# Top-k attention and two MLPs on one core: query transposes moved in the queue, a second buffer for probability halves, and the last weight's upper halves moved from GpSimd to ScalarE

## The chip, the cores and the metric

One core of a Trainium2 chip runs the whole program in one launch. The metric is the device time in microseconds (us) of one execution. Of the kernel before, three runs and one profiled execution are at hand.

## The reference, cut to what matters

```python
# attention: B=4, H=8, S=576, D=64
scores = scale * np.matmul(q, k.transpose(0, 1, 3, 2))
kth = np.partition(scores, -top_k, axis=-1)[..., -top_k:-top_k + 1]   # top_k = 32
scores = np.where(scores >= kth, scores, -1e9)
attn = np.exp(scores - max);  attn = attn / (attn.sum() + 1e-09)
x = np.matmul(attn, v)                     # -> 2304 tokens x 512
# first MLP, 512 -> 2048 -> 512
h = x @ w_in1;  x = (h * sigmoid(h)) @ w_out1
# second MLP, 512 -> 2048 -> 512
h = x @ w_in2;  out = np.where(h > 0, h, exp(min(h, 0)) - 1) @ w_out2
```

## The kernel before, in words

The work is cut into 18 chunks of 128 tokens, and each chunk into 8 attention tiles (one head, 128 queries, 576 keys), 144 tiles in all. Two of the chunks gather the 64 left-over queries of two batches; their tiles hold two heads each. Every operand of a matmul is carried as two float16 halves, an upper half `hi` and a rest `lo`, so a product is three matmuls.

A loop over slots writes out by hand, in `slot`, the program order of every engine; nothing is rescheduled. Slot s holds, for attention, the top-k of tile s on VectorE (`topk_ops`, four MAX8 and three MATCH_REPLACE8, then the mask L592), the upper probability halves of tile s-1 on ScalarE (`emit_ehi`, L618), the rests of tile s-2 on GpSimd and their transposing DMA (`emit_elo`, L624 to L627), the product with V of tile s-3 on TensorE (`emit_av`, L646), and the scores of tile s+1 on TensorE (`emit_qk`, L532). From slot 13 on a slot can also hold a quarter of a chunk's first MLP, from slot 25 on of the second, so that from then on each slot has one quarter: `emit_in` (48 matmuls, L702), `emit_act` (three or four activations on ScalarE, L716 to L724), then one slot later `emit_g` on GpSimd (L730), `emit_ghi` on ScalarE (L734) and `emit_glo` on GpSimd, and two slots later `emit_out` (12 matmuls, L750). On TensorE a slot runs: input matmuls of the MLP, product with V, output matmuls, scores of the next tile.

The names and lines that the change touches:

- `e16_p` is a pool with one buffer. `emit_ehi` writes tile t's upper halves into it, `emit_elo` the rests beside them, and the transposing DMA `et<-e16` (L627) reads both. So ScalarE's L618 of the next tile waits until that DMA has landed.
- `q_tp` (L511, L516) issues the transposing DMA `qt<-qd` for a pair of tiles from a copy of the queries in DRAM, on SP's queue, where all DMAs of the program are issued in order. It stands in the list `late[2g-3]` as a second function, which `slot` runs at the start of the slot after, behind that slot's `et` DMA.
- `kd`, `vd` and `qd` (L418, L424, L498) are the stores of split keys, values and queries to DRAM. They share one buffer, `k16_p`: ScalarE's next split into it (L389, L448, L486) waits until the store has landed.
- `w_split` makes the halves of the second MLP's output weights (weight 3, 16 blocks of 128 x 512) on GpSimd: L336 the upper half, then L164 the rest. `w_scaled` scales the block on ScalarE a slot earlier (L161). `spread` gives the slots of the blocks: slots 14 to 28 before.
- Weights live in one SBUF tile `W` of 66 rows. The raw block n lies two rows above its halves, so rows 64 and 65 are free once the last block has been split.
- The values of batch 1 are prepared `d` slots after the keys, by a table of `(r, d)`.

Of the kernel before, what the change touches and what calls it, by code (L numbers as in the profile page):

```python
# [11 lines left out]
F16 = mybir.dt.float16  # L12
# [4 lines left out]
ALU = mybir.AluOpType  # L17
# [15 lines left out]
def kernel(  # L33
# [11 lines left out]
    nc = tc.nc  # L45
    B, H, S, D = q.shape
    NT, DM = out.shape
# [15 lines left out]
    def pool(name, bufs, **kw):  # L63
        return ctx.enter_context(tc.tile_pool(name=name, bufs=bufs, **kw))
# [9 lines left out]
    e16_p = pool("e16", 1)  # L74
# [19 lines left out]
    WEND = 4 * NWP + OFF  # L94
    W = const.tile([128, WEND, 2 * DM], F16, name="W")
    Wraw = W.bitcast(F32)
    Wi = W.bitcast(I32)
    Wh = W.bitcast(BF16)

    chunks = []  # L100
    for b in range(0, B, 2):
# [58 lines left out]
    def scaled(x, s):  # L160
        nc.scalar.activation(out=x, in_=x, func=AF.Copy, scale=s)  # L161

    def sub(dst, x, hi):
        nc.gpsimd.tensor_tensor(dst, x, hi, op=ALU.subtract)  # L164
# [87 lines left out]
    def w_raw(j, n, w=None):  # L252
        return (Wraw if w is None else w)[:, j * NWP + n + OFF, :]
# [56 lines left out]
    def w_hi(j, n):  # L310
        nc.scalar.activation(out=W[:, j * NWP + n, 0:DM], in_=w_raw(j, n), func=AF.Copy, scale=sW[j][0])
# [16 lines left out]
        pmul(kc[:, 1:2], kc[:, 0:1], sW[2][1])  # L328

    def w_scaled(j, n):  # L330
        scaled(w_raw(j, n), sW[j][0])

    def w_split(j, n):
        x = j * NWP + n
        raw = w_raw(j, n)
        nc.gpsimd.tensor_scalar(W[:, x, 0:DM], raw, 1.0, 0.0, op0=ALU.mult, op1=ALU.add)  # L336
        sub(W[:, x, DM:2 * DM], raw, W[:, x, 0:DM])


    knat, vnat, qnat, kT, qT, vT, qsc = {}, {}, {}, {}, {}, {}, {}  # L340
# [273 lines left out]
    e16s = {}  # L614

    def emit_ehi(t):
        h = e16_p.tile([128, 2 * S], F16, tag="e16", name="e16")
        nc.scalar.activation(out=h[:, 0:S], in_=e32s[t], func=AF.Copy)  # L618
        e16s[t] = h

    def emit_elo(t):
        e = e32s.pop(t)
        h = e16s.pop(t)
        nc.gpsimd.tensor_tensor(h[:, S + LO:2 * S], e[:, 0:SF], h[:, 0:SF], op=ALU.subtract)  # L624
        nc.gpsimd.tensor_tensor(h[:, S:S + LO], e[:, SF:S], h[:, SF:S], op=ALU.subtract)  # L625
        et = et_p.tile([128, 2 * FC + 1, 128], F16, tag="et", name="et")
        nc.sync.dma_start_transpose(out=et, in_=h)  # L627
        ets[t] = et
# [177 lines left out]

    LDA = -99
    LDB = 28  # L810
    LAG = 13
# [10 lines left out]
    loads, sumsq, tiny, early, splits, late, low, decs = (defaultdict(list) for _ in range(8))  # L822

    def prep(slots, load, total, reduce, ops, hi, lo):
        s0, s1, s2 = slots
        if reduce and s1 >= 0:
            s0, s1 = s0 - 1, s1 - 1
        loads[s0].append(load)

        def a():  # L830
            m = total()
            if reduce:
                due.append((m, lambda m: early[s2].append(lambda: ops(m=m))))
            else:
                tiny[s2].append(ops)

        sumsq[s1].append(a)
        late[s2].append((hi, lo))

    first = {b: min(t for (bb, _), t in first_use.items() if bb == b) for b in range(B)}  # L840
    for (b, i), t in first_use.items():
        x = dict(b=b, i=i)
        if b == 0:
            prep((t - 5, t - 4, t - 3), partial(k_load, **x), partial(k_sum, **x), True,
                 partial(k_ops, **x), partial(k_hi, **x), partial(k_lo, **x))
            late[t - 2].append((partial(k_tp, **x), None))
            prep((t - 1, t, t + 1), partial(v_load, **x), partial(v_sum, **x), True,
                 partial(v_ops, **x), partial(v_hi, **x), partial(v_lo, **x))
        else:
            d, r = 4, first[b] - 35 + 8 * i + 2 * (b % 2)  # L850
            if b == 1:
                r, d = ((16, 2), (21, 3), (27, 3), (32, 3))[i]
            prep((r - 1, r + 1, r + 2), partial(k_load, **x), partial(k_sum, **x), True,
                 partial(k_ops, **x), partial(k_hi, **x), partial(k_keep, **x))
            late[t - 3].append((partial(k_tp, **x), None))
            r += d
            prep((r - 1, r + 1, r + 2), partial(v_load, **x), partial(v_sum, **x), True,
                 partial(v_ops, **x), partial(v_hi, **x, keep=True), partial(v_keep, **x))
            loads[t].append(partial(v_back, **x))
    for ch in range(NCH):  # L860
        t = ch * H
        y = t - 3
        if ch:
            y = t - 4 if ch == 1 else t - 5 if chunks[ch - 1][1] == 0 and ch > 2 else t - 8
        x = (y - 3 if ch > 1 else y - 2, y - 1, y)
        prep(x, partial(q_load, ch), partial(q_sum, ch), False,
             partial(q_ops, ch), partial(q_hi, ch), partial(q_lo, ch))
        for g in range(t // 2, (t + H) // 2):
            late[2 * g - 3].append((None, partial(q_tp, g)))

    wload, wnow = defaultdict(list), defaultdict(list)

# [2 lines left out]
    def spread(s, counts):  # L875
        return {(n, None): s + x for n, x in enumerate(x for x, c in enumerate(counts) for _ in range(c))}
# [5 lines left out]
    for j, d in dec.items():  # L882
        end = max(d.values()) + 1
        for x, s in d.items():
            decs[s].append((j, *x))
        grams[end - (j < 3)].append(j)
        traces[end + (j == 3)].append(j)
        held.add(end + (j == 3))
        if j == 3:
            for (n, _), x in spread(end + 1, (1, 1, 1, 2, 1, 2, 1, 1, 1, 1, 1, 1, 0, 1, 1)).items():  # L890
                late[x].append((partial(w_scaled, j, n), None))
                splits[x + 1].append(partial(w_split, j, n))
            continue
        ends.append(end)
# [45 lines left out]
    def slot(s):  # L940
# [25 lines left out]

        if LDA <= s < LDB:
            for f in loads[s - 1]:
                f()
        if 0 <= s - 2 < NTILE:  # L970
            emit_elo(s - 2)
        if not LDA <= s < LDB:
            for f in loads[s - 1]:
# [50 lines left out]
        if 0 <= s - 1 < NTILE:  # L1024
            emit_ehi(s - 1)
# [84 lines left out]
```

## Time and profile before

| | |
|---|---|
| median of 3 runs | 1146.91 us (1146.54 to 1148.77) |
| the profiled execution | 1149.13 us, span 1147.4 us |
| PE busy | 1011.7 us, 88% of the span |
| DVE busy | 952.2 us, 83% |
| ACT busy | 874.8 us, 76% |
| POOL busy | 820.7 us, 72% |
| DMA queue of the program | 387008 packets, 139.39 MB |

PE is TensorE's matmuls, PEld its weight loads, DVE is VectorE, ACT ScalarE, POOL GpSimd, and SP the engine whose queue issues the DMAs; SPq is that queue, and L12 is line 12 of the kernel. A row of a list of waits says which instruction waited for which, the time in total, how often and the longest. In a timeline a bracket gives the engine's idle time ahead of the instruction, and what ended it.

### The profile page before, as it was taken

How to read it: one execution, taken by the hardware profiler on the slowest of the kernel's cores; microseconds unless marked ns; L12 is line 12 of the kernel's file. 1: busy time of each engine (PE TensorE's matmuls, PEld its weight loads, DVE VectorE, ACT ScalarE, POOL GpSimd, SP SyncE). 2: the span in 40 equal slices, each digit the busy share in tenths (PEclk: the TensorE clock that was granted, in tenths of full speed). 3: DMA queues.
4: the chain of work that ended last, by engine and by line, in shares of the span. 5: the costliest groups of instructions: out<-in, count | busy, mean ns of one | idle time of the engine just before them, and what ended most of it. 6: DMA issues, size and time to landing. Idle time of an engine off the chain costs nothing.

```text
span 1147.4 us, 31015 instructions
## 1 busy us (share of the span) xinstructions
PE 1011.7 (88%) x11974; PEld 723.8 (63%) x11974; DVE 952.2 (83%) x2215; ACT 874.8 (76%) x1568; POOL 820.7 (72%) x1026
## 2 busy tenths in 40 slices
PE   0166779689999999999999999999999999999997
PEld 0123426376677676777777776767677777777765
DVE  5998998999798989999998989989889999994000
ACT  5566887789887888888888888877777778776654
POOL 5877875898877676777768776777667677767543
PEclk9978999899999999999999999999999999999999
DMA  9978792555688654646778565638665545433100
GB/s 308 298 211 244 237 227 48 110 115 100 127 159 158 106 121 92 129 96 119 119 138 158 98 117 101 120 83 135 109 127 84 94 84 88 83 61 61 29 13 17
DMA packets 387156, 141.37 MB, mean 123 GB/s; under 512 B 362944, under 2 KB 370112, under 8 KB 387008
## 3 DMA queue, kind: packets, MB, share of 16 engines
q1 hardware_dynamic: 387008, 139.39, 58.9%
q8 instruction: 94, 1.54, 0.6%
q14 instruction: 54, 0.44, 0.1%
HBM read 52.17 MB, written 21.10 MB: 64 GB/s over the span
## 4 chain that ended last, share of the span: by engine, by line
PE 29%; POOL 23%; DMA 12%; issue 11%; ACT 7%; SPq 2%; DVE 1%; POOLq 0%; ACTq 0%
PE h L702 13%; PE a L750 12%; DMA et<-e 8%; POOL e L624 7%; POOL t L730 6%; POOL gh L164 4%; PE S L532 2%; PE av L646 2%; POOL e L625 2%; ACT gh L734 1%; POOL x L164 1%; DMA qt<-qd 1%; POOL v L164 1%; DMA vd<-v 1%; ACT e L618 1%
## 5 line engine op out<-in xcount | busy, mean ns | idle before, releaser
L702 PE MATMUL h<-xt,W 128*128 128x128 f16 x6912 | 410.5, 219 | 2.0 <-DMA xt<-x 2.0
L750 PE MATMUL a<-W,gh 128*128 128x512 f16 x1728 | 402.6, 383 | 9.8 <-ACT o L796 4.9
L702 PEld LDWEIGHTS <-W 128*128 128x128 f16 x6912 | 395.6, 98 | 13.2 <-issue 2.8
L564 DVE MAX8 m<-r 128x8 f32<-128x576 f32 x432 | 312.7, 749 | 2.2
L750 PEld LDWEIGHTS <-gh 128*128 128x128 f16 x1728 | 160.5, 99 | 188.0 <-issue 11.5
L624 POOL TENSOR_TENSOR e<-e,e 128x512 f16<-128x512 f32 x144 | 166.9, 1159 | 137.5 <-ACT e L618 126.4
L164 POOL TENSOR_TENSOR gh<-t,gh 128x512 f16<-128x512 f32 x144 | 167.1, 1160 | 69.1 <-ACT gh L734 69.1
L568 DVE MATCH_REPLACE8 r<-m,r 128x576 f32<-128x576 f32 x288 | 213.7, 742 | 0.0
L730 POOL TENSOR_TENSOR t<-u,t 128x512 f32<-128x512 f32 x144 | 183.0, 1271 | 29.4 <-ACT u L724 23.1
L734 ACT ACTIVATE gh<-t 128x512 f16<-128x512 f32 x144 | 90.3, 627 | 119.1 <-POOL t L730 117.9
L564 DVE MAX8 m<-S 128x8 f32<-128x576 f32 x144 | 109.6, 761 | 56.5 <-PE S L532 55.9
L532 PE MATMUL S<-kt,qt 128*128 128x288 f16 (+1 forms) x640 | 98.7, 295 | 50.5 <-DVE sv L136 21.1
L579 ACT ACTIVATE e<-S,bias,c 128x576 f32<-128x576 f32 x144 | 119.7, 831 | 25.8 <-DVE r L568 18.7
L618 ACT ACTIVATE e<-e 128x576 f16<-128x576 f32 x144 | 97.5, 677 | 47.8 <-DMA et<-e 25.7
L532 PEld LDWEIGHTS <-qt 128*128 128x128 f16 (+1 forms) x640 | 55.9, 102 | 120.4 <-issue 23.8
L592 DVE SCALAR_TENSOR_TENSOR e<-S,m,e 128x576 f32<-128x576 f32 x144 | 115.3, 800 | 0.1
L568 DVE MATCH_REPLACE8 r<-m,S 128x576 f32<-128x576 f32 x144 | 107.5, 747 | 0.0
L646 PE MATMUL av<-vt,et 128*128 128x64 f16 (+1 forms) x2240 | 91.9, 195 | 16.3 <-DMA et<-e 15.8
L646 PEld LDWEIGHTS <-et 128*128 128x128 f16 (+1 forms) x2240 | 80.3, 102 | 27.4 <-DMA et<-e 21.1
L317 PE MATMUL lo<-W,eye 128*128 128x512 f32 x96 | 58.5, 694 | 20.0 <-ACT W L322 19.1
L280 POOL TENSOR_TENSOR W<-W 128x512 int32<-128x512 int32 (+1 forms) x55 | 69.0, 1278 | 9.3 <-DVE W L277 3.5
L724 ACT ACTIVATE u<-u,c 128x512 f32<-128x512 f32 x72 | 58.6, 814 | 2.4
(125 smaller groups left out, 1165.0 us busy)
## 6 DMA issues: line engine op xcount, KB each, us to landing
W<-in_moe_w_in_dram SPq DMA_DIRECT2D x32, 512.0 KB, 7.1
W<-in_moe_w_out_dram SPq DMA_DIRECT2D x22, 512.0 KB, 6.2
qd<-q SPq DMA_DIRECT2D x34, 256.0 KB, 4.3
kn<-in_k_dram SPq DMA_DIRECT2D x16, 288.0 KB, 4.1
qn<-in_q_dram SPq DMA_DIRECT2D x16, 256.0 KB, 3.6
out_dram<-o SPq DMA_DIRECT2D x16, 256.0 KB, 2.8
vd<-v SPq DMA_DIRECT2D x12, 320.0 KB, 4.3
vt<-vd SPq DMA_DIRECT2D x24, 160.0 KB, 2.7
```

What stands on the lines that cost most here:

```text
L164: nc.gpsimd.tensor_tensor(dst, x, hi, op=ALU.subtract)
L532: nc.tensor.matmul(out=ps[n * e:n * e + n, a, 0:HALF], lhsT=qt[:, 2 * (t % 2) + p, n * e:n * e + n], rhs=kt[:, a * HALF:(a + 1) * HALF], s ...
L564: nc.vector.max(st["m8"][:, i, :], src if i == 0 else st["r"])
L568: nc.vector.match_replace(out=fold(r) if i == 0 else r, in_to_replace=st["m8"][:, i, :], in_values=src if i == 0 else r, imm_value=LOW,)
L579: nc.scalar.activation(out=fold(e), in_=src, func=AF.Exp, scale=c[:, 0:1], bias=bias)
L592: nc.vector.scalar_tensor_tensor(e, src, st["m8"][:, n - 1, 7:8], e, op0=ALU.is_ge, op1=ALU.mult, accum_out=acc)
L618: nc.scalar.activation(out=h[:, 0:S], in_=e32s[t], func=AF.Copy)
L624: nc.gpsimd.tensor_tensor(h[:, S + LO:2 * S], e[:, 0:SF], h[:, 0:SF], op=ALU.subtract)
L646: nc.tensor.matmul(out=o, lhsT=et[:, c, n * e:n * e + n], rhs=r, start=(i == 0), stop=(i == len(seq) - 1))
L702: nc.tensor.matmul(out=ps[:, f:f + 128], lhsT=w, rhs=xt[:, z, :], start=(kk == 0 and x == 0), stop=(kk == KDM - 1 and x == 2),)
L730: nc.gpsimd.tensor_tensor(t, u, t, op=ALU.add if l else ALU.mult)
L750: nc.tensor.matmul(out=acc, lhsT=gh[:, z, u * 128:(u + 1) * 128], rhs=W[:, n, w * 512:(w + 1) * 512], start=(m == 0 and x == 0), stop=(m = ...
```

## The change

Four edits, of which the first three go by tables of slots and lists.

1. Query transposes of the pairs g > 4 are issued at the end of slot 2g-3, and no longer at the start of slot 2g-2.
2. Odd tiles from tile 31 on write their probability halves into rows 64 and 65 of `W` (`spare`) and not into the one buffer of `e16_p`, which leaves that buffer to the even tiles.
3. The upper halves of weight 3 are made by `w_hi` on ScalarE (L311, with the scale in it), in the slot of `w_scaled` and just ahead of it; L336 on GpSimd goes. The blocks are spread over slots 14 to 25, two in some.
4. The values of batch 1, heads 4 and 5, are prepared one slot later.

```diff
+    spare = W[:, WEND - 2:WEND, :].rearrange("p a x -> p (a x)")
...
     def w_scaled(j, n):
+        w_hi(j, n)
         scaled(w_raw(j, n), sW[j][0])
 
     def w_split(j, n):
         x = j * NWP + n
-        raw = w_raw(j, n)
-        nc.gpsimd.tensor_scalar(W[:, x, 0:DM], raw, 1.0, 0.0, op0=ALU.mult, op1=ALU.add)
-        sub(W[:, x, DM:2 * DM], raw, W[:, x, 0:DM])
+        sub(W[:, x, DM:2 * DM], w_raw(j, n), W[:, x, 0:DM])
...
     def emit_ehi(t):
-        h = e16_p.tile([128, 2 * S], F16, tag="e16", name="e16")
+        if t % 2 and t > TWO:
+            h = spare[:, 0:2 * S]
+        else:
+            h = e16_p.tile([128, 2 * S], F16, tag="e16", name="e16")
...
+    TWO = 30
...
-                r, d = ((16, 2), (21, 3), (27, 3), (32, 3))[i]
+                r, d = ((16, 2), (21, 3), (27, 4), (32, 3))[i]
...
-            late[2 * g - 3].append((None, partial(q_tp, g)))
+            late[2 * g - 3].append((partial(q_tp, g), None) if g > H // 2 else (None, partial(q_tp, g)))
...
-            for (n, _), x in spread(end + 1, (1, 1, 1, 2, 1, 2, 1, 1, 1, 1, 1, 1, 0, 1, 1)).items():
+            for (n, _), x in spread(end + 1, (2, 1, 2, 2, 2, 1, 2, 0, 1, 1, 1, 1)).items():
                 late[x].append((partial(w_scaled, j, n), None))
                 splits[x + 1].append(partial(w_split, j, n))
```

On SP's queue, around tiles 80 to 83 (chunk 10, in the middle of the program), the rows before: `et` is the transposed probabilities, `qt` the transposed queries, `xt` the MLP's transposed input, `kd` the stored keys.

```order
L627 DMA_TRANSPOSE et<-e_10328 128x9x128
L511 DMA_TRANSPOSE qt<-qd 128x4x128
L681 DMA_TRANSPOSE xt<-x_10447 128x8x128
L627 DMA_TRANSPOSE et<-e_10451 128x9x128
L627 DMA_TRANSPOSE et<-e_10576 128x9x128
...
L418 DMA kd<-k_10587 128x1152
L511 DMA_TRANSPOSE qt<-qd 128x4x128
L627 DMA_TRANSPOSE et<-e_10707 128x9x128
```

And the same place now:

```order
L630 DMA_TRANSPOSE et<-e_10303 128x9x128
L684 DMA_TRANSPOSE xt<-x_10422 128x8x128
L630 DMA_TRANSPOSE et<-W 128x9x128
L511 DMA_TRANSPOSE qt<-qd 128x4x128
L630 DMA_TRANSPOSE et<-e_10550 128x9x128
...
L418 DMA kd<-k_10561 128x1152
L630 DMA_TRANSPOSE et<-W 128x9x128
L511 DMA_TRANSPOSE qt<-qd 128x4x128
```

Each `qt` has moved: it stood behind an even tile's `et` and the stores of that slot, and stands now behind an odd tile's `et`. The transpose that followed `kd` in the first piece is, for its pair of tiles, the one ahead of `et<-e_10550` in the second. Odd tiles' `et` read `W`.

On ScalarE, behind the upper probability halves of tile 19 (slot 20, in the stretch where weight 3 is split), the rows before:

```order
L618 ACTIVATE e_2561<-e_2474 128x576
L161 ACTIVATE vn<-vn,sv 128x640
L448 ACTIVATE v_2576<-vn 128x10x64
L161 ACTIVATE W<-W,sw 128x512
L577 ACTIVATE bias<-m_2642,fixed,c 128x1
L579 ACTIVATE e_2649<-S,bias,c 128x576
```

And now:

```order
L621 ACTIVATE e_2567<-e_2483 128x576
L162 ACTIVATE vn<-vn,sv 128x640
L448 ACTIVATE v_2582<-vn 128x10x64
L312 ACTIVATE W<-W,sw 128x512
L162 ACTIVATE W<-W,sw 128x512
L312 ACTIVATE W<-W,sw 128x512
L162 ACTIVATE W<-W,sw 128x512
L577 ACTIVATE bias<-m_2651,fixed,c 128x1
L579 ACTIVATE e_2658<-S,bias,c 128x576
```

Three weight instructions more stand between tile 19's upper halves and tile 21's exponentials.

## Rows read from the trace of the kernel before

**Rows 1.** The page's part 2: the span in 40 slices, TensorE

```profile
PE   0166779689999999999999999999999999999997
```

**Rows 2.** Windows: length, then busy us (count) of PE, PEld, DVE, ACT, POOL; clock

```profile
0.00:245.00 245.00, 144.60 (x1186) 86.63 (x1187) 223.13 (x507) 171.93 (x316) 184.50 (x231) 0.91 0.77 204
311.00:1041.00 730.00, 708.73 (x8980) 525.84 (x8979) 667.32 (x1560) 587.39 (x1052) 524.44 (x670) 1.00 0.61 111
```

**Rows 3.** The chain that ended last: start, us, what; two output steps of the MLP

```profile
862.76 2.59 PE a L750 x12
...
868.95 2.59 PE a L750 x12
```

**Rows 4.** Waits of PE from 311 to 1041 us

```profile
PE av L646 <- DMA et<-e: 12.2, 13, 2.4
PE S L532 <- DMA qt<-qd: 5.6, 7, 1.7
PE a L750 <- ACT o L796: 2.9, 5, 0.8
```

**Rows 5.** Waits of ACT from 311 to 1041 us

```profile
ACT gh L734 <- POOL t L730: 86.7, 73, 1.9
ACT e L618 <- DMA et<-e: 15.4, 17, 3.9
ACT q L486 <- DMA kd<-k: 7.4, 4, 3.0
...
ACT q L486 <- DMA vd<-v: 6.5, 3, 2.3
```

**Rows 6.** L627, the transposing DMA of the probabilities, from 311 to 1041 us

```profile
DMA to landing us min/median/max: 3.2/3.3/5.1
```

**Rows 7.** Timeline of SP's queue around tile 74: start, us, what

```profile
601.65 1.29 SPq L627 DMA_TRANSPOSE et<-e  x1
...
605.70 1.25 SPq L511 DMA_TRANSPOSE qt<-qd  x1
```

**Rows 8.** Timeline of PE just behind it

```profile
610.21 0.67 PE L532 MATMUL S<-kt,qt 128*128 128x288 f16 x4 [1.67 <-DMA qt<-qd]
```

**Rows 9.** Timeline of PE at tile 97

```profile
759.05 0.85 PE L646 MATMUL av<-vt,et 128*128 128x64 f16 x14 [2.38 <-DMA et<-e]
759.72 4.17 PE L750 MATMUL a<-W,gh 128*128 128x512 f16 x12
```

**Rows 10.** Windows, the same columns, at that place

```profile
759.00:762.00 3.00, 2.94 (x20) 1.55 (x21) 1.33 (x3) 2.85 (x6) 2.15 (x3) 0.53 0.00 0
```

**Rows 11.** Groups of instructions: shapes, count | busy us, mean ns | idle before

```profile
L311 ACT ACTIVATE W<-W,sw 128x512 f16<-128x512 f32 x48 | 31.9, 719 | 0.0
...
L336 POOL TENSOR_SCALAR W<-W 128x512 f16<-128x512 f32 x16 | 9.9, 619 | 0.0
```

**Rows 12.** Windows of ACT alone: length, busy us (count), clock, DMA

```profile
187.00:236.00 49.00, 32.48 (x59) 0.86 0.51 101
```

**Rows 13.** Timeline of ACT at tiles 18 to 20

```profile
224.87 0.67 ACT L618 ACTIVATE e<-e 128x576 f16<-128x576 f32 x1
...
230.57 0.68 ACT L618 ACTIVATE e<-e 128x576 f16<-128x576 f32 x1 [0.29 <-DVE z L143]
...
235.77 0.71 ACT L161 ACTIVATE W<-W,sw 128x512 f32<-128x512 f32 x1
...
239.17 0.69 ACT L618 ACTIVATE e<-e 128x576 f16<-128x576 f32 x1
```

**Rows 14.** Timeline of PE at tile 20

```profile
244.72 0.58 PE L646 MATMUL av<-vt,et 128*128 128x64 f16 x14 [0.25 <-DMA et<-e]
...
246.71 2.33 PE L750 MATMUL a<-W,gh 128*128 128x512 f16 x10 [0.98 <-POOL gh L164]
```

**Rows 15.** Timeline of DVE a slot later

```profile
249.57 0.77 DVE L564 MAX8 m<-S 128x8 f32<-128x576 f32 x1 [1.00 <-PE S L532]
```

**Rows 16.** Timeline of PE in slot 31

```profile
301.61 4.44 PE L750 MATMUL a<-W,gh 128*128 128x512 f16 x12 [1.98 <-ACT o L796]
```

## The prediction

> **What bounds the kernel now.** I read the page's slices first: from about 230 us to the end TensorE's digit is 9 nearly throughout [rows 1]. The windows cut the span there. Up to 245 us DVE is busy 223.1 of 245 us, PE 144.6; from 311 us (tile 31) to 1041 us PE is busy 708.7 of 730, DVE 667.3 and ACT 587.4 [rows 2]. So there are two stages: the first goes at the pace of DVE's top-k, the second at TensorE's. In the chain of waits two output steps of the MLP follow each other in 6.19 us [rows 3]; where nothing disturbs TensorE, that is the length of a slot, and this change takes none of its matmuls away.
>
> What can be gained in the second stage is therefore what TensorE stands idle there: 730 - 708.7 = 21.3 us. The list of its waits names nearly all of it: 12.2 us for transposed probabilities, 5.6 for transposed queries, 2.9 for ScalarE's output copy, which frees the accumulator [rows 4]. One loss lies beside these. After the longest idle time, 2.38 us at tile 97, the granted clock was 0.53 for the next 3 us, between the two levels of 1.2 and 2.4 GHz, and the output step took 4.17 us, not 2.59 [rows 3, 9, 10]: 1.6 us more.
>
> The judgement that TensorE is the bound there can be doubted, since a busy share counts pipelined matmuls as full. The Trainium skill says so (Perfetto Trace Analysis, Identifying the Most-Contended Engine): judge TensorE's headroom by the share of weight loads. That is 525.8 of 730, 72% [rows 2], and would leave some 200 us of room. The undisturbed slots of 6.19 us speak against it, and they decide: I cap the gain at the idle time.
>
> **Edit 2, the second buffer.** It adds no instruction. ScalarE waited 15.4 us in 17 places for the last `et` to land before it could write the next upper halves [rows 5]. With alternating buffers it waits for the DMA of two tiles ago, a slot of 6.2 us earlier, against a flight of 3.2 to 5.1 us [rows 6]; those 15.4 us go. But ScalarE's far longer wait is for GpSimd, 86.7 us for `t` [rows 5]: upper halves, rests on GpSimd, `t`, `gh` and the activations form a ring through both engines that a buffer does not shorten. Part of TensorE's 12.2 us comes from the buffer, part from that ring and from slow transposes. Bounds: 0 and 12.2 us; I take 7, a little over half, since the stalls that cost ScalarE most (3.9 us the longest) are the buffer's. Of the clock's 1.6 us I take 1. ScalarE's output copy stands right behind the upper halves in its slot, so an earlier ScalarE frees the accumulator earlier: of 2.9 us I take 2 (bounds 0 and 2.9).
>
> **Edit 1, the query transposes.** Before, `qt` stands behind an `et` that waits for GpSimd, then behind loads and a store: at tile 74 it went out 4.05 us after that `et` [rows 7], and TensorE waited 1.67 us for it [rows 8]. It is now issued a whole `et` earlier, about 6.2 us, and the longest of these waits was 1.7 us [rows 4]. Its buffer is long free, since the scores that last read it were made a slot before. I take 5 of the 5.6 us (bounds 0 and 5.6).
>
> It has a price. It leaves an even tile's `et` and the stores `kd` and `vd`, and comes behind an odd tile's `et`. ScalarE's 13.9 us of waits for those two stores [rows 5] should shrink, which I leave within the 7 above. The odd `et` right after a chunk's start is one that TensorE waits for, and is now followed at once by another transpose. The trace does not show this pair. Its nearest rows bound what an `et` can lose: nothing, or 5.1 - 3.3 = 1.8 us [rows 6]. I take 0.25 us, near the median and not the longest, since two issues of 1.29 and 1.25 us [rows 7] put the second transpose some 2.5 us into a flight of 3.3. Some 13 chunks: 3 us lost. Where there was no stall, this costs nothing.
>
> The Trainium skill (DMA: Bandwidth & Descriptors, Issuing engines are not separate DMA queues) says that all DMAs run on the same 16 engines and interleave. By that rule the collision is only moved from even tiles to odd ones, and the saving would be nearer the third rival below than to mine; rows 6 shows that flights do stretch, but not by whom.
>
> **Edit 3, upper halves on ScalarE.** Off GpSimd go 16 instructions, 9.9 us; onto ScalarE go 16 of 0.719 us, 11.5 us [rows 11], all in slots 14 to 25, and in most of slots 14 to 20 three more in a row. GpSimd's saving is covered by its own waits. ScalarE's addition is not free: by the order, 15 of the 16 fall between 187 and 236 us, 10.8 us against 49 - 32.5 = 16.5 us of idle time there [rows 12], and part of that idle time is waiting that stays (for `et`, whose buffer is single until tile 31, and for stores). Follow tile 20: three more instructions stand at 235.77 us, 2.2 us, on top of 1 to 2 us of backlog, my estimate from the same rows. Its upper halves then start not at 239.17 us but 3 to 4 later [rows 13], and so does its `et`, for which TensorE already waits at 244.72 [rows 14]. The scores behind are waited for by DVE at 249.57 [rows 15], so this lies on the path: 3 to 4 us lost.
>
> Most is given back: from slot 26 on ScalarE has no weight work and GpSimd's slots 28 and 29 have none, and in slot 31 TensorE loses 1.98 us to a late output copy and 4.44 - 2.59 = 1.85 us in the step behind it [rows 3, 16]. Bounds: 5 lost, 4 gained; I take 1.5 lost. DVE's work is untouched.
>
> **Edit 4** moves one preparation by a slot; the work and its engines are the same. With edits 1 and 3 before 311 us it is inside the bounds just given. The early query transposes (before 187 us) lie under DVE's 223 us [rows 2]; if that cover went, they would cost one issue of 1.25 us each [rows 7] on SP.
>
> **The sum.** Gained 7 + 1 + 2 + 5 = 15, lost 3 + 1.5 = 4.5: 10.5 us. The profiled execution took 1149.13 us, 2.2 above the median; 1149.13 - 10.5 = 1138.6, and on the median 1146.91 - 10.5 = 1136.4 us.
>
> **The rivals**, on the median's scale.
>
> Full relief: the ring keeps pace once the buffer is gone, and all idle time that the rows name goes, 12.2 + 5.6 + 2.9 + 1.6 = 22.3 us, with the first stage even: 1124.6 us. For it: undisturbed slots run at 6.19 us. Against: the 86.7 us ring. If the weight-load rule of the skill were right, the gain could go beyond the cap; I give that no more than this rival's chance. 0.14.
>
> The ring bounds: the second buffer only moves ScalarE's wait from `et` to `t`. Then only the 5 us for queries are saved, less 1.5: 1143.4 us. For it: 86.7 against 15.4 us [rows 5]. 0.20.
>
> The collision eats it: each chunk's odd `et` loses about 0.9 us, 13 x 0.9 = 11.7 instead of 3, and the sum is 15 - 11.7 - 1.5 = 1.8 us gained: 1145.1 us, no change. 0.06.
>
> Slower: the odd `et` of each chunk stretches by the full 1.8 us, 13 x 1.8 = 23.4 us, on TensorE's path. 15 - 23.4 - 1.5 = -9.9: 1156.8 us. It decides from (15 - 1.5) / 13 = 1.04 us a chunk on. Against: the median flight of 3.3 us lies by the shortest, though many DMAs are in flight. 0.08, with ScalarE's 11.5 us falling wholly on the path counted in.
>
> That the change doesn't do what it says would need `spare` to wait for TensorE's reads of `W`; by the program order an odd tile's upper halves still wait for a DMA and for DVE alone. No chance of its own.
>
> **How the numbers follow.** A measurement of this kernel can tell 0.2%, 2.3 us, from no change. My forecast has 0.52; with full relief and the ring rival, both faster, 0.86; same 0.06, slower 0.08. The forecast's own bounds are about 1127 to 1143. The range 1124 to 1145 reaches from full relief over the ring rival to the edge of no change, and leaves out the slower cases, part of the same ones and the forecast's tails, under 2 in 10.
>
> **What would show it.** Right: ScalarE's wait for `et` after 311 us near zero; TensorE's wait for `qt` gone; its wait for `et` from 12.2 to some 5 to 8 us; a stall of 3 to 4 us at tile 20 and none in slot 31. Wrong: `et` flights on odd tiles above 4 us in the median, TensorE's wait for `et` unchanged, or a second stage that takes much more or less than the 730 - 12 = 718 us that the sum gives it.

## The result, and the profile after

The changed kernel took 1134.81 us (median of 5 runs, 1133.99 to 1139.16) against 1146.91 of the kernel before: ratio 0.9887, 95% interval 0.9863 to 0.9911. 10.5 us had been predicted, 12.1 came. In a second measurement (below, g4_after) the ratio was 0.9897. The profiled execution took 1133.99 us, span 1132.3; it is the fastest of the five and that of before lies above its median, so the two traces differ by 15.1 us where the medians differ by 12.1.

First the stage that TensorE sets. The window has the columns of [rows 2]:

```profile
311.00:1025.00 714.00, 703.53 (x8980) 525.44 (x8979) 665.55 (x1556) 585.76 (x1052) 525.57 (x671) 1.00 0.60 113
```

As many matmuls, 8980, as took a window of 730 us now fit into one of 714, and TensorE stands idle for 10.5 us in it, not 21.3. Where it still waits (waits of PE from 311 to 1025 us; nothing lies between 1025 and 1041):

```profile
PE av L649 <- DMA et<-W: 7.4, 9, 1.7
PE av L649 <- DMA et<-e: 2.3, 4, 1.4
PE a L753 <- ACT o L799: 0.8, 2, 0.4
```

Against [rows 4]: the wait for queries is gone, that for probabilities went from 12.2 to 9.7 us, that for ScalarE's output copy from 2.9 to 0.8. And of ScalarE, first of before (311 to 1041 us, a line that [rows 5] leaves out), then of after (311 to 1025 us):

```profile
ACT e L579 <- DVE r L568: 7.3, 12, 1.1
```

```profile
ACT gh L737 <- POOL t L733: 68.4, 66, 1.9
ACT e L579 <- DVE r L568: 19.9, 25, 1.1
```

The line on `et` is no longer in this list at all: 15.4 us gone, as forecast. The wait for GpSimd, which was to hold the ring together, fell too, from 86.7 to 68.4 us. What grew is ScalarE's wait for VectorE's top-k, from 7.3 to 19.9 us.

Now the chain of waits in this stage, its shares by line, first of before (311 to 1041 us), then of after (311 to 1025 us); the view ends its line there:

```profile
by line: PE h L702 14.0%; PE a L750 13.5%; issue 12.8%; DMA et<-e 11.3%; POOL e L624 8.7%; POOL t L730 6.6%; POOL gh L164 5.0%; PE S L532 2.7%; PE av L646 2.7%; POOL e L625 2.1%; ACT gh L734 1.8%; DMA qt<-qd 1.7%; POOL x L164 1.4%; POOL v L
```

```profile
by line: PE a L753 22.1%; PE h L705 21.5%; issue 10.5%; POOL gh L165 6.0%; POOL t L733 5.2%; PE av L649 4.9%; PE S L532 4.3%; POOL W L627 3.0%; POOL e L627 2.8%; DMA et<-W 2.4%; DMA et<-e 2.1%; DMA kd<-k 1.2%; POOL x L165 1.1%; DVE r L568 1
```

The `et` transposes' part of the chain shrank from 11.3% to 4.5%, and that of TensorE's four lines grew from 32.9% to 52.8%. A slot in which nothing disturbs TensorE has the length it had [rows 3]; the chain of after:

```profile
856.95 2.59 PE a L753 x12
863.11 2.59 PE a L753 x12
```

6.16 us. TensorE was the bound, and the kernel is closer to it now. (The weight-load rule of the Trainium skill, Perfetto Trace Analysis, Identifying the Most-Contended Engine, had left some 200 us of room. This trace does not bear it out: in the 6.16 us from 856.95 on TensorE never stands, and weight loads are busy for 4.66 of them.)

TensorE's places in time (timeline of PE, after): the product with V of tile 20, the output step of slot 31, the product of tile 31, tile 97 with its output step, and the product of tile 142.

```profile
248.36 0.58 PE L649 MATMUL av<-vt,et 128*128 128x64 f16 x14 [1.24 <-DMA et<-e]
...
304.10 2.75 PE L753 MATMUL a<-W,gh 128*128 128x512 f16 x12 [1.25 <-ACT o L799]
...
323.36 0.57 PE L649 MATMUL av<-vt,et 128*128 128x64 f16 x14
...
749.56 0.57 PE L649 MATMUL av<-vt,et 128*128 128x64 f16 x14
749.96 2.75 PE L753 MATMUL a<-W,gh 128*128 128x512 f16 x12
...
1034.81 0.57 PE L649 MATMUL av<-vt,et 128*128 128x64 f16 x14
```

The same in the kernel before, tiles 31 and 142:

```profile
322.15 0.57 PE L646 MATMUL av<-vt,et 128*128 128x64 f16 x14
...
1049.60 0.57 PE L646 MATMUL av<-vt,et 128*128 128x64 f16 x14
```

Tile 20 comes 248.36 - 244.72 = 3.64 us later than before [rows 14] (3 to 4 were forecast). At tile 31 1.21 us of that are left. Slot 31 still waits for ScalarE, 1.25 us and not 1.98, but its step takes 2.75 us, not 4.44 [rows 16]. From tile 31 to tile 142 it is 711.45 us against 727.45: 16.0 us gained. Windows of these two stretches, before and after:

```profile
322.15:1049.60 727.45, 706.17 (x8960) 524.69 (x8958) 659.53 (x1537) 583.85 (x1044) 520.80 (x664) 1.00 0.60 110
```

```profile
323.36:1034.81 711.45, 701.21 (x8960) 524.49 (x8958) 658.96 (x1537) 581.43 (x1044) 523.10 (x665) 1.00 0.60 113
```

Idle time fell by 11.0 us, of which the lists of waits name 20.7 - 10.5 = 10.2 (rows above and [rows 4]). The other 5.0 us are busy time of the same 8960 matmuls. Some 1.6 of it is clock at tile 97, where the 2.38 us stall and the half clock behind it [rows 9, 10] are gone; the rest, over 3 us, no list names.

### The profile page after: what moved, and what is told of

Same layout as the page of the kernel before. It is cut to its first block, busy times and chain, and to the rows that moved or that the text cites. A ratio compares the mean times of both kernels' runs of the same rounds, so it can differ in the third digit from the quotient of the medians.

```text
span 1132.3 us, 31066 instructions
## 1 busy us (share of the span) xinstructions
PE 1006.5 (89%) x11974; PEld 724.3 (64%) x11974; DVE 952.1 (84%) x2215; ACT 883.0 (78%) x1584; POOL 811.3 (72%) x1010
## 4 chain that ended last, share of the span: by engine, by line
PE 43%; POOL 20%; issue 12%; DVE 10%; ACT 7%; DMA 7%; SPq 1%; POOLq 0%; ACTq 0%; DVEq 0%
PE a L753 18%; PE h L705 17%; POOL gh L165 5%; POOL t L733 5%; PE av L649 3%; PE S L532 3%; POOL e L627 3%; DVE m L564 3%; DVE y L275 2%; DVE r L568 2%; DMA et<-e 2%; POOL W L627 2%; DMA et<-W 1%; DVE W L278 1%; PE lo L318 1%
## 5 line engine op out<-in xcount | busy, mean ns | idle before, releaser
L705 PEld LDWEIGHTS <-W 128*128 128x128 f16 x6912 | 395.9, 98 | 15.4 <-issue 5.1
L753 PE MATMUL a<-W,gh 128*128 128x512 f16 x1728 | 397.4, 379 | 4.7 <-ACT o L799 2.1
L627 POOL TENSOR_TENSOR e<-e,e 128x512 f16<-128x512 f32 x87 | 101.0, 1161 | 98.7 <-ACT e L621 95.2
L627 POOL TENSOR_TENSOR W<-e,W 128x512 f16<-128x512 f32 x57 | 66.2, 1161 | 27.6 <-ACT W L621 25.5
L621 ACT ACTIVATE e<-e 128x576 f16<-128x576 f32 x87 | 58.8, 676 | 28.1 <-DMA et<-e 12.7
L318 PE MATMUL lo<-W,eye 128*128 128x512 f32 x96 | 61.9, 732 | 19.2 <-ACT W L323 18.3
```

What stands on the lines that cost most here:

```text
L705: nc.tensor.matmul(out=ps[:, f:f + 128], lhsT=w, rhs=xt[:, z, :], start=(kk == 0 and x == 0), stop=(kk == KDM - 1 and x == 2),)
L753: nc.tensor.matmul(out=acc, lhsT=gh[:, z, u * 128:(u + 1) * 128], rhs=W[:, n, w * 512:(w + 1) * 512], start=(m == 0 and x == 0), stop=(m = ...
```

## The experiments

All ratios are against the kernel before, run beside them; intervals are 95%.

| run | edits | median us | ratio (interval) |
|---|---|---|---|
| e1_queries | 1 | 1155.45 | 1.0052 (1.0038 to 1.0066) |
| e2_buffer | 2 | 1134.59 | 0.9874 (0.9860 to 0.9888) |
| e3_split | 3 | 1153.24 | 1.0033 (1.0018 to 1.0047) |
| e4_no_split | 1, 2 | 1133.48 | 0.9864 (0.9850 to 0.9879) |
| g1_queries_3 | 1, third `qt` buffer | 1155.90 | 1.0047 (1.0028 to 1.0066) |
| g2_both_3 | 1, 2, third `qt` buffer | 1135.68 | 0.9877 (0.9857 to 0.9896) |
| g3_needed | 2, 1 for g % 4 = 3 | 1132.45 | 0.9852 (0.9832 to 0.9872) |
| g4_after | the change, again | 1138.35 | 0.9897 (0.9879 to 0.9915) |
| h1_skip_head | 1 without g % 4 = 2 | 1150.86 | 1.0011 (0.9996 to 1.0026) |
| h2_needed | g3 again | 1133.03 | 0.9856 (0.9829 to 0.9884) |
| h3_buffer | e2 again | 1135.21 | 0.9872 (0.9847 to 0.9896) |
| h4_both | e4 again | 1133.52 | 0.9866 (0.9836 to 0.9895) |

The e, g and h runs each shared their runs of the kernel before (medians 1148.74, 1149.84 and 1148.98 us). Repeats agree within 0.001.

### Each part alone

**The query transposes alone (e1_queries).**

```diff
-            late[2 * g - 3].append((None, partial(q_tp, g)))
+            late[2 * g - 3].append((partial(q_tp, g), None) if g > H // 2 else (None, partial(q_tp, g)))
```

> Edit 1 alone: the query transposes are issued at the end of their slot, one buffer for the probability halves, weight 3 split as before. My theory (two causes that each take their own part of TensorE's idle time): TensorE's 5.6 us of waits for qt go, its waits for et stay at 12 us or grow by 1 to 3 us because an odd et is now followed by another transpose; 3 to 5 us gained, 1142 to 1144 us. Rival 1 (the ring through ScalarE and GpSimd sets the pace, and only the queries matter): nearly the whole 12 us of the full change, 1135 to 1138 us. Rival 2 (the transposes' collision on odd tiles is what counts): no gain or a loss, 1146 to 1150 us, with TensorE's wait for et at 18 us or more.

The edit to which I had given 5 us less 3 makes the kernel 6 us slower. Waits of PE, 311 to 1025 us:

```profile
PE av L646 <- DMA et<-e: 20.3, 16, 3.5
```

The 5.6 us of waits for queries went, and the waits for probabilities grew from 12.2 to 20.3; those for ScalarE's output copy are 4.4 us. The largest is at tile 72. SP's queue there, in the kernel before and then in this one:

```profile
584.63 4.32 SPq L408 DMA_TRANSPOSE kt<-kd  x2
589.12 1.28 SPq L627 DMA_TRANSPOSE et<-e  x1
590.44 1.31 SPq L511 DMA_TRANSPOSE qt<-qd  x1
```

```profile
592.08 3.35 SPq L408 DMA_TRANSPOSE kt<-kd  x2
595.54 1.20 SPq L511 DMA_TRANSPOSE qt<-qd  x1
596.91 1.24 SPq L627 DMA_TRANSPOSE et<-e  x1
```

At a chunk's start two transposes of keys stand ahead of `et`, and the moved `qt` has joined them. TensorE, same run:

```profile
600.23 0.58 PE L646 MATMUL av<-vt,et 128*128 128x64 f16 x14 [3.49 <-DMA et<-e]
```

3.49 us of wait at a flight of 3.3 us: the transpose was not slow, it was issued late. The next largest stalls, 2.67 and 2.48 us, are at tiles 32 and 104. These chunks are the two with the left-over queries, whose query transpose takes two issues (L516), 2.48 us at tile 32. At tile 104, behind `kt`, before and then in this run:

```profile
801.00 1.28 SPq L627 DMA_TRANSPOSE et<-e  x1
802.33 3.51 SPq L516 DMA_TRANSPOSE qt<-qd  x2
```

```profile
802.95 3.22 SPq L516 DMA_TRANSPOSE qt<-qd  x2
806.33 1.30 SPq L627 DMA_TRANSPOSE et<-e  x1
```

And before the queue there is a wait that the kernel before did not have. The order of SP's queue with its semaphores, a `qt` of before and one of after:

```
L511 DMA_TRANSPOSE qt<-qd 128x4x128 [waits DMAHW5_49]
L511 DMA_TRANSPOSE qt<-qd 128x4x128 [waits DMAHW5_49,PE_49]
```

A slot earlier, the transpose must wait until TensorE has done with the buffer. Waits of SP from 311 to 1030 us in this run, two of the six lines of L511 and L516, 28.8 us in all, none before:

```profile
SPq L511 <- PE av L646: 12.3, 9, 2.1
SPq L511 <- PE h L702: 7.8, 7, 1.7
```

So there were three candidates: this wait, the place in the queue, and the flights.

**The second buffer alone (e2_buffer).**

```diff
+        if t % 2 and t > TWO:
+            h = spare[:, 0:2 * S]
+        else:
+            h = e16_p.tile([128, 2 * S], F16, tag="e16", name="e16")
```

> Edit 2 alone: the second buffer from tile 31 on. My theory: ScalarE's 15.4 us of waits for et after 311 us go, TensorE's waits for et fall from 12 to about 5 us, those for qt shrink a little because the et ahead in SP's queue goes out earlier; 6 to 9 us gained, 1138 to 1141 us. Rival 1 (the ring sets the pace, the buffer only moves ScalarE's wait from et to GpSimd): 1145 to 1147 us, ScalarE's wait for t growing by about 15 us from 86.7. Rival 3 (the two edits only work together, since the chain runs through whichever is left): under 2 us gained alone.

14 us, more than the theory gave it: as much as the whole change. Waits of PE, 311 to 1025 us:

```profile
PE S L533 <- DMA qt<-qd: 4.8, 6, 1.4
PE av L650 <- DMA et<-W: 4.6, 4, 2.3
PE av L650 <- DMA et<-e: 0.2, 1, 0.2
```

The wait for probabilities fell from 12.2 to 4.8, ScalarE's copy is gone from the list, the queries are nearly as they were. Of the three lines 20.7 us [rows 4] became 9.6. From tile 31 to tile 142:

```profile
320.70:1033.68 712.98, 703.22 (x8960) 524.03 (x8958) 658.80 (x1537) 581.60 (x1044) 521.97 (x664) 1.00 0.62 112
```

14.5 us less than before, 11.5 of them idle time and 3.0 busy time of as many matmuls. None of it is clock: the stall at tile 97 stands in this run too, 2.30 us, and the clock fell behind it (0.51 from 749 to 752 us).

**The split on ScalarE alone (e3_split).**

```diff
+        w_hi(j, n)
         scaled(w_raw(j, n), sW[j][0])
...
-        nc.gpsimd.tensor_scalar(W[:, x, 0:DM], raw, 1.0, 0.0, op0=ALU.mult, op1=ALU.add)
```

> Edit 3 alone: upper halves of weight 3 on ScalarE, slots 14 to 25, one buffer and the old place of the query transposes. My theory: TensorE waits 3 to 4 us more for et at tile 20, slot 31 gives back 2 to 3 us; 0 to 3 us lost, 1147 to 1150 us. Rival (GpSimd's 9.9 us are what bounded slots 15 to 29, so that edit 3 brings a part of the gain): 1142 to 1145 us.

3.8 us slower, a little past the theory's 3. TensorE's products with V of tiles 20, 31 and 142:

```profile
249.43 0.58 PE L645 MATMUL av<-vt,et 128*128 128x64 f16 x14 [1.45 <-DMA et<-e]
...
325.39 0.57 PE L645 MATMUL av<-vt,et 128*128 128x64 f16 x14
...
1054.00 0.57 PE L645 MATMUL av<-vt,et 128*128 128x64 f16 x14
```

Late by 4.71 us at tile 20, by 3.24 at tile 31, by 4.40 at tile 142: what the stage with the weights loses is given back only in part. That is clear of scatter: in the three traces with edit 3 tile 20 comes at 248.02 to 249.43 us and tile 31 at 322.87 to 325.39, in the eleven without it at 243.47 to 246.52 and 320.12 to 322.23.

**Edits 1 and 2 (e4_no_split).** The two diffs above together.

> Edits 1 and 2 together, without edits 3 and 4. My theory: the parts add, 11 to 14 us gained, 1133 to 1136 us, which is the full change or up to 2 us faster than it; no new stall at tile 20, the stall of 2 us in slot 31 is back. Rival (edit 3 brings a part of the gain): slower than the full change by 2 to 5 us, 1137 to 1140 us. Rival 3 (edits 1 and 2 work only together): 1133 to 1136 us, but with e1 and e2 each under 2 us.

0.9864, and 0.9866 in h4_both, beside 0.9887 and 0.9897 of the full change: edits 3 and 4 cost 2.6 and 3.6 us here as well. Each pair of intervals overlaps, but both pairs, e3_split and the places of tile 31 say the same.

### Why the query transposes cost

**A third buffer for the queries (g1_queries_3, g2_both_3).**

```diff
+        if g > 17 and g % 3 == 0:
+            qt = spare[:, 2 * S:2 * S + 512].rearrange("p (a x) -> p a x", a=4)
+        else:
+            qt = qt_p.tile([128, 4, 128], F16, tag="qt", name="qt")
```

> Edit 1 alone, with a third buffer for the transposed queries of the pairs from g = 18 on, in the free columns of rows 64 and 65 of W. Edit 1 alone took 1155.45 us, about 6 us more than the kernel before. Theory (the queue is held): moved ahead, each query transpose has to wait on SP's queue until TensorE's scores free its buffer, 29 us in all between 311 and 1030 us, and the next tile's et stands behind it. A third buffer takes this wait away: SP's wait for TensorE at L515 near zero, TensorE's wait for et from 20.3 to 13 to 16 us, and the time 1149 to 1152 us; a part of 1 to 3 us stays, since at tiles 72 and 104 the issue of 1.3 us itself stands ahead of an et that is late. Rival (the transposes disturb each other in flight, the prediction's collision): the third buffer changes nothing, 1154 to 1156.5 us, et waits of 19 to 21 us.

> Edits 1 and 2 with the third buffer for transposed queries. Edits 1 and 2 alone took 1133.48 us, with 10.0 us of TensorE's waits for et. Theory (the queue is held): 1130 to 1132 us, et waits of 6 to 8 us, no wait of SP for TensorE at the query transposes. Rival (collision in flight, or the issue alone): 1132.5 to 1134.5 us, et waits of 9 to 11 us.

The theory fell. In neither run does SP's list name a wait of a query transpose for TensorE any more, and the times did not move: 1.0047 beside 1.0052, 0.9877 beside 0.9864 (with 1135.68 us the second even lies above its rival's range). 28.8 us of waits on a queue had cost nothing that can be measured: SP had time. In g1_queries_3 TensorE still waits 19.4 us for `et`, and at tile 72 the queue looks as in e1_queries: two `kt`, the `qt`, then the `et`, 4.85 us behind the start of `kt` (595.76 - 590.91; 4.83 in e1_queries). Without any wait of `qt`, its own issue and the two of `kt` put the `et` where it was.

**Without the pairs at a chunk's start (h1_skip_head).**

```diff
+            late[2 * g - 3].append((partial(q_tp, g), None) if g > H // 2 and g % 4 != 2 else (None, partial(q_tp, g)))
```

> Edit 1 alone without the pairs whose moved transpose stands ahead of the first et of a chunk (g % 4 = 2), the e16 buffer single. Edit 1 alone lost 6 us; a third buffer for the queries took SP's wait for TensorE away and the loss stayed. Theory now (issue time on SP's queue): the loss is made at the first tile of a chunk (32, 72, 104), whose et stands behind two transposes kt and the moved qt and goes out 4.3 to 6.6 us after its upper halves began. Without these pairs it goes out as before: TensorE's et waits 12 to 14 us in place of 20, no wait for qt, and 1144 to 1149 us beside 1148 to 1150 of the kernel before. Rival (flights stretched by the transposes behind them, at the tiles 8n+1): the loss stays, 1153 to 1157 us.

The loss fell from 6 us to 1.3 (1.0011; the intervals of the two runs do not touch), a little above the 1144 to 1149 us expected. The place is right: `et` of tile 72 stands directly behind `kt` again,

```profile
589.62 3.38 SPq L408 DMA_TRANSPOSE kt<-kd  x2
593.16 1.28 SPq L627 DMA_TRANSPOSE et<-e  x1
```

and TensorE's stalls at tiles 32, 72 and 104 went from 2.67, 3.49 and 2.48 us to none, 2.07 and 0.71. All traces together say the same of the queue. From the start of the upper halves to the issue of their `et` it takes, in the seven runs in which all pairs moved, 4.0 to 5.1 us at tile 32, 6.0 to 6.7 at tile 72 and 5.0 to 6.6 at tile 104; in the seven others 2.2 to 2.3, 4.4 to 5.4 and 2.4 to 3.3.

But one expectation missed: the sum of TensorE's `et` waits stayed.

```profile
PE av L646 <- DMA et<-e: 20.2, 18, 2.3
```

More and shorter ones came elsewhere (1.81 and 2.03 us at tiles 34 and 35). Nor does the clock make up the difference. In e1_queries it fell behind tiles 32 and 104, in h1_skip_head behind tile 97 (windows, clock third from the end; two of e1_queries, then one of h1_skip_head):

```profile
331.40:334.40 3.00, 2.94 (x32) 1.82 (x33) 1.54 (x6) 2.87 (x7) 2.14 (x3) 0.60 0.67 143
809.60:812.60 3.00, 2.83 (x31) 1.97 (x32) 1.28 (x2) 2.40 (x5) 2.03 (x3) 0.54 0.33 61
```

```profile
761.00:764.00 3.00, 2.96 (x22) 1.42 (x23) 1.60 (x7) 2.86 (x6) 2.17 (x3) 0.71 0.00 0
```

So the two profiled executions, 3.7 us apart in span, differ by only 1.4 us from tile 31 to tile 142 (732.33 and 730.91 us), which is about what one fall costs by [rows 9], and by 1.7 us behind tile 142, where the mean clock is 0.98 and 1.00. That the moved transposes at a chunk's start cost most of the 6 us is shown by the times; how those microseconds add up is not shown by these two traces.

**Only the pairs that TensorE waits for (g3_needed, h2_needed).** In e2_buffer all six waits for queries are at the last pair of tiles of a chunk (g % 4 = 3).

```diff
+            late[2 * g - 3].append((partial(q_tp, g), None) if g > 20 and g % 4 == 3 else (None, partial(q_tp, g)))
```

> Edit 2, and edit 1 for one pair of tiles in four only: the third pair after each chunk's start (g % 4 = 3, from g = 23 on), the only ones whose transposed queries TensorE waited for (4.8 us in six places with edit 2 alone, at 1134.59 us). Theory (the price of edit 1 is the order on SP's queue at the other pairs): those 4.8 us go and nothing comes in their place, et waits stay at 5 us, 1130 to 1132 us. Rival (collision): the moved transposes now start just behind the et of tiles 8n+1, the ones that TensorE waits for (4.6 us); these flights stretch and the et waits grow to 8 to 10 us, 1133 to 1135 us.

> Edit 2 with edit 1 for g % 4 = 3 from g = 23 on, again, beside edit 2 alone and edits 1 and 2. Theory: the order needed < buffer alone, by 1.5 to 3.5 us, since 4.8 us of waits for queries go and 1.5 to 3 us of waits for et come at the tiles 8n+1; ratio to the kernel before 0.984 to 0.9865. Rival: the same as the buffer alone within 1 us.

Waits of PE, 311 to 1025 us, g3_needed:

```profile
PE av L650 <- DMA et<-W: 7.1, 5, 2.5
PE a L754 <- ACT o L800: 1.8, 3, 0.8
PE av L650 <- DMA et<-e: 0.5, 2, 0.3
```

The 4.8 us for queries are gone and 2.8 us of `et` and 1.8 of ScalarE's copy have come: net about nothing by these lists. The waits for `et<-W` lie at tiles 8n+1, whose transposes are followed by the moved `qt`: 7.1 and 8.1 us in two runs, against 4.6 and 5.0 in the two with the buffer alone. That is the collision of the prediction, of its size: some 3 us over 13 chunks. The flights show it too: at the tiles 8n+1 from 33 on the median is 3.65 and 3.59 us in these two runs, 3.25 and 3.28 with the buffer alone. Where all pairs moved, the odd tiles (`et<-W`) take longer and the even ones (`et<-e`), which no `qt` follows any more, less time; median us to landing, 311 to 1041 us, e2_buffer and then e4_no_split:

```profile
et<-W SPq DMA_TRANSPOSE x57, 3.3
et<-e SPq DMA_TRANSPOSE x56, 3.4
```

```profile
et<-e SPq DMA_TRANSPOSE x57, 3.2
et<-W SPq DMA_TRANSPOSE x57, 3.4
```

By the ratios g3_needed and h2_needed were 2.5 and 1.8 us below the buffer alone, within the intervals, so I do not call that gain shown. This kernel is the fastest of all by its medians, and lies clear of the full change: in the same group of runs 1131.30 to 1135.06 against 1136.33 to 1139.74 us.

**The repeats.**

> The change as it is, beside the others on one chip, to read what edits 3 and 4 cost on top of edits 1 and 2 (1133.48 us then). Theory (ScalarE's added work costs 3 us where it stands, and part comes back in the second stage): 1134.5 to 1136.5 us, above edits 1 and 2 by 1 to 3. Rival (edit 3 pays for itself beside the buffer): 1132.5 to 1134 us.

> Edit 2 alone, again: ratio to the kernel before 0.986 to 0.989, as measured before (0.9874), and 1.5 to 3.5 us above the kernel with the needed query transposes moved.

> Edits 1 and 2, again: ratio 0.985 to 0.988 as before (0.9864); by the theory within 1.5 us of edit 2 alone, since what edit 1 saves at the tiles that waited for queries it gives back at tiles 32 to 35, 72 and 104. Rival (edit 1 is worth its own 3 us beside the buffer): 3 us below edit 2 alone.

The full change came out at 1138.35 us on a chip on which the kernel before took 1149.84, by ratio 3.6 us above h4_both, a little past the theory's 1 to 3. Edits 1 and 2 were by ratio 1.1 and, again, 0.7 us below the buffer alone, within the intervals; edit 1's own 3 us did not show.

## Why the prediction was right, and where its steps were not

The time lay 1.6 us below the forecast and well in the range, and the sign was right. The steps deserve less credit: that the sum came so close is in part luck, since edit 2 gave 4.5 us more than was taken, and the other edits together some 3 less.

**Edit 2, mis-sized.** 7 + 1 + 2 = 10 us were taken; the buffer alone gave 14.5 (0.9874 of 1148.7). The named parts were close: 7.4 us of `et` waits (7 taken), 2.9 of the output copy (all of it, by the list; 2 taken) and 0.8 of queries. The 1 us of clock did not come: in e2_buffer the clock fell at tile 97 as before. What was missed is TensorE's busy time, 3.0 us less for the same matmuls. The cap itself ("I cap the gain at the idle time") was thus too tight: a stall also costs in the matmuls beside it. An undisturbed output step takes 2.75 us in a timeline and 2.59 in the chain, where the next matmuls begin before its end; if each stall undoes one such overlap of 0.16 us, the 14 fewer waits of the lists (25 and 11) make 2.2 us. That is my estimate. The same difference lies in the 1.6 us of the prediction, which set 4.17 us of a timeline against 2.59 of the chain; against 2.75 the step at tile 97 is 1.4 us too long.

**The ring.** ScalarE's 86.7 us of waiting for GpSimd was no bound of its own. When the buffer came free they fell to 68.4 (63.7 in e2_buffer), and TensorE's waits fell with them. ScalarE waited for VectorE instead. A long wait in that list can be time that the engine has to spare. The ring rival, at 0.20, stood too high; e2_buffer alone rules it out.

**Edit 1, the step that failed.** The saving was right as a wait (5.6 us, gone in every run in which all pairs moved) and wrong as time. "Its buffer is long free" was not so: the changed order has a wait for TensorE that the one before lacked, and I could have read it there. That wait turned out harmless. The price that I worked out, a collision of flights behind odd tiles, exists at about its size (0.25 us taken, 0.3 to 0.4 in the medians at tiles 8n+1), and the even tiles' flights became shorter. The price that I left out is on SP's queue at the head of a chunk: one issue of 1.3 us, at tiles 32 and 104 two of 2.5 and 3.2 us together, more ahead of an `et` that two `kt` had already delayed. I looked at the `et` ahead of `qt` and not at the one behind.

With one buffer this price can run on: a late `et` holds ScalarE's next upper halves, hence the next `et`. ScalarE waited 21.3 us for `et` in e1_queries, 15.4 before. With two that path is gone. In the changed kernel the `et` of tile 72 goes out just as long behind its upper halves (6.3 us in both), and TensorE waits 1.43 us there in place of 3.49; it is not always so, since g4_after still stalls for 3.11 us at tile 104. That this path makes the whole difference is my reading. The difference itself is measured: the terms were no sum, for edit 1 costs 6 us alone and is worth 0 to 1 beside edit 2.

**Edit 3, a bit worse.** 1.5 us were taken, from bounds of 5 lost to 4 gained; 3.8 were lost alone and, with edit 4, 2.6 and 3.6 beside edits 1 and 2. The chain through tile 20 was right step by step: ScalarE's upper halves of tile 20 start at 242.86 us, 3.69 later than in [rows 13],

```profile
242.86 0.69 ACT L621 ACTIVATE e<-e 128x576 f16<-128x576 f32 x1
```

and DVE waits for the scores of a slot later:

```profile
252.06 0.77 DVE L564 MAX8 m<-S 128x8 f32<-128x576 f32 x1 [1.56 <-PE S L532]
```

at 252.06 against 249.57, 1.56 us for 1.00 [rows 15]. At tile 20 itself TensorE stalls for 1.24 us; the rest of the 3.64 had built up before. The stall in slot 31 shrank, but the room that it gave did not hold all of the loss.

**Edit 4** has no run of its own; g4_after and e4_no_split bound it together with edit 3.

**The signs.** Of those named, ScalarE's wait for `et` went, so did TensorE's for `qt`, and the stage took 714 us (718 forecast). TensorE's wait for `et` fell to 9.7 us and not to 5 to 8, there was no stall of 3 to 4 us at tile 20, and slot 31 kept 1.25 us.

**The rivals.** Full relief, 1124.6 us, was missed mainly by the 9.7 us of waits for `et` that stayed. The third and fourth rivals put 0.9 and 1.8 us on each chunk's odd `et`; the flights stretched by 0.3 to 0.4. The sign of the fourth came true for edit 1 alone; the buffer, which that rival kept at its 10 us, outweighed it.

## What to carry to other kernels

A transfer moved earlier on an in-order queue is paid for by the transfer that it now precedes: look there first, at the place where that queue is fullest, and move only those transfers that somebody waits for. A single buffer whose release runs through a DMA can pass a delay on that queue from tile to tile; a second one can pay for more than the waits that name it (14.5 us here, where the lists lost 11.1). Waits of an engine or a queue that has time to spare (28.8 us here) can be removed without any effect that shows: test a suspected wait by itself before blaming it.

## What the runs showed of the hardware

The clock does not follow from the length of the last stall alone. At tile 72, e1_queries and g1_queries_3 stalled for 3.49 and 3.52 us. The 3 us behind (windows, clock third from the end), in the first and in the second run:

```profile
600.00:603.00 3.00, 2.77 (x25) 1.50 (x26) 1.16 (x4) 2.41 (x5) 1.97 (x3) 1.00 0.48 93
```

```profile
599.00:602.00 3.00, 2.96 (x20) 1.59 (x21) 0.98 (x4) 2.41 (x5) 2.17 (x3) 0.50 0.42 80
602.00:605.00 3.00, 3.00 (x12) 1.21 (x11) 0.00 (x0) 2.46 (x5) 1.63 (x2) 0.61 1.05 123
```

One went on at the upper level, the other fell to the lower (1.2 GHz) for most of 6 us. Within e1_queries, too, the clock fell behind the shorter stalls at tiles 32 and 104 (2.67 and 2.48 us, windows above) and not behind the 3.49. The same stall can so cost its own length or more than that, and part of the scatter between executions may come from it; no run here tests that.
